# Pooled sums on VectorE alone, three products cut in two, and a new order of steps in a fused attention and two-mixer kernel

## The chip, the core and the metric

The kernel runs on one core of a Trainium2 chip. TensorE (PE), VectorE (DVE), ScalarE (ACT) and GpSimd (POOL) each work through a queue of their own in order; SyncE (SP) issues most DMA transfers, POOL the accumulating ones. Times are device microseconds of one execution; the kernel's time is the median of three.

## What is computed

Local and pooled attention on 4 batches of 8 heads, 576 positions and width 64, then a channel mix, then a gated layer with a convolution over three positions:

```python
q_d = q.reshape(B, H, Sd, factor, D).mean(axis=3)      # factor 4; k_d, v_d alike
out_d = sm_attn(q_d, k_d, v_d)
out_up = np.repeat(out_d, factor, axis=2)
mask = np.abs(pos[:, None] - pos[None, :]) < factor
scores = np.where(mask, scale * q @ k.T, -1e9)
x = out_up + softmax(scores) @ v

xk = mu_k * x + (1.0 - mu_k) * x_prev                  # xr alike, with mu_r
k = np.maximum(xk @ w_k, 0.0)
v = k * k @ w_v
x = sigmoid(xr @ w_r) * v

h = np.maximum(x @ w_in, 0.0)
conv_out = sum(conv_w[k] * hp[:, k:k + S, :] for k in range(3))
out = h * sigmoid(conv_out) @ w_out
```

The model is 512 wide and 1024 in the inner layer. All is float32.

## The kernel before

**Phase one.** Attention goes by groups of four heads (two groups a batch). A group of batch 0 is done in two halves (blocks 0 to 9 and 10 to 17), one of the later batches at once. Its steps are: load keys and queries (`kq`) and values (`vw`); sums of four neighbouring positions of keys and queries (`pooled_kq`, lines 501 to 525, tiles `kqd`); local scores (L549, L558) with maximum, exponential, sum and normalisation on DVE and ACT (L574 to L596); pooled scores (L623) with theirs (L640 to L667); transposes (L699, L750); outputs (L718, L769); and an addition of both on DVE (L784) that frees the PSUM bank of L769. PSUM for scores and outputs of attention is two tiles, `a20` and `a21`, used in turns.

The mix multiplies each chunk of positions by w_k and w_v. The first chunk (288 positions of batch 0) runs in plain f32 on weights as they arrive (L871 for w_k, L901 for w_v, on tiles `st_f`). For all later chunks each float32 operand is split into a rounded part and the rest, and a product is three matmuls (high by high, low by high, high by low): L935 with w_k, L985 with w_v. A weight tile is loaded in a transposed form of its bits: ACT cuts it (L398, L399), DVE puts it together (L380, L383), then its high part is written by ACT or DVE (L419 or L421, the function `high`) and its low part by DVE (L425). `mix_prep` makes the operand of a chunk (L832 on ACT, L840 on DVE, then the split at L849 and L854).

**Phase two** takes six chunks of 384 positions: gates with w_r (L1268), whose results are split into x1 (L1293 on ACT, L1295 on DVE), eight products with w_in (`hidden`, L1309; first result to ACT, L1337 to L1342), the convolution and its gate on DVE and ACT (L1354 to L1376), and the output with w_out (`outp`, L1389).

**What sets the order.** The program first records steps, each with an engine, what it reads and writes, and a function that issues its instructions. The list `ORDER` then gives the sequence in which all 1655 steps are issued, so it fixes each engine's queue and SP's and POOL's DMA queues too. `SECOND` names the steps that may run on two engines and take the second one: for the pooled sums of batches 1 to 3 `both = ("DVE", "POOL")`, for roundings and squares `("ACT", "DVE")`. Nine of the twelve pooled sums of batches 1 to 3 are in `SECOND`. On POOL such a sum is three additions:

```python
eng.tensor_tensor(out=o, in0=i[:, :, 0], in1=i[:, :, 1], op=ALU.add)
for j in range(2, FAC):
    eng.tensor_tensor(out=o, in0=o, in1=i[:, :, j], op=ALU.add)
```

Of the kernel before, what the change touches and what calls it, by code (L numbers as in the profile page):

```python
# [14 lines left out]
ALU = mybir.AluOpType  # L15
# [195 lines left out]
def pool(n):  # L211
    return 0.2 + 1.8e-3 * n
# [6 lines left out]
TAIL = 0.165  # L219
# [3 lines left out]
def tile_local_attention__then__channel_mix__then__conv_glu(  # L223
# [209 lines left out]
    def group(b, gp):  # L433
# [66 lines left out]
        def pooled_kq(i0, i1):  # L500
# [3 lines left out]
            for pr in range(2):  # L504
                t, k = g["kq"][0][:, pr], g["kq"][1]
                d, dk = g["kqd"][0][:, pr], g["kqd"][1]

                def f(eng, t=t, d=d):
                    o = d[:, a // FAC:e // FAC]
                    i = t[:, a:e].rearrange("p (s t) -> p s t", t=FAC)  # L510
                    if eng is nc.vector:
# [979 lines left out]
```

## Time and profile before

| | |
|---|---|
| median of 3 runs | 568.85 us (568.65 to 570.09) |
| the profiled execution | 568.25 us |
| its span in the trace | 566.5 us |
| PE busy | 547.7 us, 97% |
| DVE busy | 397.6 us, 70% |
| ACT busy | 307.2 us, 54% |
| POOL busy | 57.6 us, 10% |
| moved by DMA | 66.20 MB |

The span is the time from the first to the last instruction of one execution. The page of the profile also cuts the span into 40 slices of 14.16 us and gives for each the busy share of every engine and the granted clock of TensorE in tenths. A line of a timeline has the start, the time taken, the engine, the source line, the operation, the tiles written and read, the count, and in brackets the idle time ahead with what ended it. PE's waits give engine, line, what was waited for, the total, the times and the longest.

### The profile page before, as it was taken

What the parts mean: (1) busy time and instruction counts of PE and PEld (TensorE: products, weight loads), DVE (VectorE), ACT (ScalarE), POOL (GpSimd) and SP (SyncE); (2) the same over time, 40 slices, a digit from 0 to 9 for tenths busy, and PEclk for the clock granted to TensorE, in tenths of its full rate; (3) what the DMA queues carried; (4) which work ended last, traced back from release to release, by engine and by line L of the source; (5) the groups of instructions that cost most, each with busy time, mean ns of one, the idle gap of its engine ahead of it and who ended that gap; (6) DMA issues with size and microseconds to landing.
All of it is one profiled execution on the core that took longest, in us unless ns stands there. A gap on an engine that the chain in (4) does not pass through costs nothing.

```text
span 566.5 us, 13091 instructions
## 1 busy us (share of the span) xinstructions
PE 547.7 (97%) x5412; PEld 496.8 (88%) x5412; DVE 397.6 (70%) x758; ACT 307.2 (54%) x715; POOL 57.6 (10%) x159
## 2 busy tenths in 40 slices
PE   5898989999999999999999999999999999999996
PEld 3676768899988989999999998998998999999985
DVE  5989896774858575666456799677677777765770
ACT  4666866565644574663565764555445355453441
POOL 6023031511052100000000000000000000000000
PEclk9989997999999999999999999999999999999999
DMA  8545956383545373342205420303031200000011
GB/s 349 211 165 156 335 173 197 105 311 105 192 139 189 93 235 132 107 181 75 106 1 181 152 103 2 113 0 113 0 94 50 83 23 34 1 38 20 1 39 73
DMA packets 26396, 66.20 MB, mean 117 GB/s; under 512 B 2656, under 2 KB 12384, under 8 KB 25312
## 3 DMA queue, kind: packets, MB, share of 16 engines
q1 hardware_dynamic: 24608, 62.41, 31.5%
q0 software_dynamic: 1728, 2.95, 3.2%
q8 instruction: 42, 0.69, 0.5%
q14 instruction: 18, 0.15, 0.1%
HBM read 51.20 MB, written 14.16 MB: 115 GB/s over the span
## 4 chain that ended last, share of the span: by engine, by line
PE 78%; DVE 12%; DMA 3%; ACT 3%; issue 2%; POOL 1%; ACTq 0%; DVEq 0%; POOLq 0%; SPq 0%
PE a L1389 17%; PE mm L935 15%; PE mm L985 14%; PE mm L1309 8%; PE a L1309 8%; PE a L1268 5%; PE mm L1268 4%; DMA st_d<-in_moe_w_v 2%; PE a L769 2%; PE a L558 1%; PE a L750 1%; PE a L718 1%; PE a L699 1%; DVE st_f L380 1%; DVE st_f L383 1%
## 5 line engine op out<-in xcount | busy, mean ns | idle before, releaser
L1389 PE MATMUL a<-wk,wv 128*128 128x512 f32 x432 | 100.5, 390 | 0.0
L935 PE MATMUL mm<-xk,wk 128*128 128x432 f32 (+1 forms) x480 | 94.5, 353 | 0.7 <-ACT tmp L919 0.7
L1389 PEld LDWEIGHTS a<-wk,wv 128*128 128x128 f32 x432 | 81.0, 188 | 15.9
L985 PE MATMUL mm<-k,wv 128*128 128x432 f32 (+1 forms) x480 | 91.1, 347 | 0.0
L935 PEld LDWEIGHTS mm<-xk,wk 128*128 128x128 f32 x480 | 86.0, 193 | 4.5 <-ACT tmp L919 1.0
L985 PEld LDWEIGHTS mm<-k,wv 128*128 128x128 f32 x480 | 84.2, 188 | 3.6 <-issue 0.4
L1309 PE MATMUL mm<-k,wi 128*128 128x386 f32 x288 | 54.4, 340 | 0.7 <-ACT k L1293 0.7
L1309 PE MATMUL a<-k,wi 128*128 128x386 f32 x288 | 54.4, 340 | 0.0
L1309 PEld LDWEIGHTS mm<-k,wi 128*128 128x128 f32 x288 | 51.3, 189 | 1.9 <-ACT k L1293 1.0
L1309 PEld LDWEIGHTS a<-k,wi 128*128 128x128 f32 x288 | 51.4, 189 | 0.3
L1364 ACT ACTIVATE tmp<-tmp 128x384 f32<-128x384 f32 x48 | 24.8, 524 | 46.5 <-DVE tmp L1358 46.4
L954 ACT ACTIVATE tmp<-mm 128x432 f32<-128x432 f32 (+1 forms) x40 | 20.2, 508 | 25.4 <-PE mm L935 20.8
L380 DVE SCALAR_TENSOR_TENSOR st_f<-st_f,st_d 128x512 uint32<-128x512 uint32 x28 | 21.1, 752 | 18.2 <-ACT st_d L399 18.2
L1367 DVE SCALAR_TENSOR_TENSOR tmp<-tmp,h 128x384 f32<-128x384 f32 x48 | 26.3, 556 | 10.7 <-ACT tmp L1364 9.2
L1376 DVE TENSOR_TENSOR wv<-tmp,wv 128x384 fp32r<-128x384 f32 x48 | 25.9, 553 | 11.1 <-ACT wv L1374 11.0
L1374 ACT CAST wv<-tmp 128x384 fp32r<-128x384 f32 x48 | 24.0, 511 | 13.9 <-DVE tmp L1367 13.6
L1358 DVE SCALAR_TENSOR_TENSOR tmp<-h,cw_sb,tmp 128x384 f32<-128x384 f32 x48 | 29.7, 619 | 2.5
L974 DVE TENSOR_TENSOR k<-tmp,k 128x432 fp32r<-128x432 f32 (+1 forms) x40 | 22.8, 579 | 12.3 <-ACT k L966 11.6
L1355 DVE SCALAR_TENSOR_TENSOR tmp<-h,cw_sb,tmp 128x384 f32<-128x384 f32 x48 | 29.7, 619 | 2.5
L1268 PE MATMUL mm<-xk,wr 128*128 128x386 f32 x144 | 27.0, 340 | 0.3 <-ACT h L1337 0.3
L1268 PE MATMUL a<-xk,wr 128*128 128x386 f32 x144 | 26.7, 339 | 0.0
L1354 DVE TENSOR_SCALAR tmp<-h,cw_sb 128x384 f32<-128x384 f32 x48 | 20.0, 416 | 9.3 <-ACT h L1339 5.8
(165 smaller groups left out, 853.8 us busy)
## 6 DMA issues: line engine op xcount, KB each, us to landing
vw<-in_vw SPq DMA_DIRECT2D x7, 1152.0 KB, 9.0
kq<-in_kq SPq DMA_DIRECT2D x6, 1152.0 KB, 7.1
x_d<-xT SPq DMA_DIRECT2D x16, 288.0 KB, 5.6
out_dram<-xT SPq DMA_DIRECT2D x18, 256.0 KB, 2.0
st_d<-in_moe_w_k SPq DMA_DIRECT2D x8, 512.0 KB, 4.5
st_d<-in_moe_w_v SPq DMA_DIRECT2D x8, 512.0 KB, 5.4
st_d<-in_moe_w_in SPq DMA_DIRECT2D x8, 512.0 KB, 5.4
st_d<-in_moe_w_out SPq DMA_DIRECT2D x8, 512.0 KB, 3.9
```

Source lines behind the costliest of these rows:

```text
L380: nc.vector.scalar_tensor_tensor(out=f, in0=f, scalar=3, in1=low, op0=ALU.logical_shift_left, op1=ALU.bitwise_or)
L935: nc.tensor.matmul(pst[:, 0:n], lhsT=wk_t[wt][:, kt, mt * P:(mt + 1) * P], rhs=late["xk"][:, xs, kt, 0:n], start=(kt == 0 and g == 0), sto ...
L985: nc.tensor.matmul(pst[:, 0:n], lhsT=wv_t[wt][:, kt, mt * P:(mt + 1) * P], rhs=late["k2"][xs][:, at[kt], 0:n], start=(kt == 0 and g == 0), ...
L1268: nc.tensor.matmul(pst[:, 0:CW], lhsT=late["wr"][wt][:, kt, mt * P:(mt + 1) * P], rhs=r_t(xs)[:, kt, :], start=(kt == 0 and g == 0), stop= ...
L1309: nc.tensor.matmul(pst[:, 0:CW], lhsT=late["wi"][wt][:, kt, mt * P:(mt + 1) * P], rhs=x1s(xs)[:, kt, :], start=(kt == 0 and g == 0), stop= ...
L1355: nc.vector.scalar_tensor_tensor(out=cv, in0=tap(0), scalar=cw[:, 0, mt:mt + 1], in1=cv, op0=ALU.mult, op1=ALU.add)
L1358: nc.vector.scalar_tensor_tensor(out=cv, in0=tap(2), scalar=cw[:, 2, mt:mt + 1], in1=cv, op0=ALU.mult, op1=ALU.add)
L1364: step("ACT", act(CH), lambda: nc.scalar.activation(cv, cv, AF.Tanh, scale=0.5), (), [cvk])
L1367: lambda: nc.vector.scalar_tensor_tensor(out=gt, in0=cv, scalar=1.0, in1=tap(1), op0=ALU.add, op1=ALU.mult),
L1374: step("ACT", act(CH), lambda: nc.scalar.copy(gh, gf), ["wv_old", gk], [("gh", j)])
L1376: ("DVE",), (0.56,), lambda e: e.tensor_sub(gl, gf, gh.bitcast(F32)),
L1389: nc.tensor.matmul(pst, lhsT=xs[:, tt * P:(tt + 1) * P], rhs=wo[wt][:, kt, :], start=(kt == 0 and g == 0), stop=(kt == KF - 1 and g == 2),)
```

## The change

`pooled_kq` loses its form for POOL: all sums of four are one `reduce_sum` on DVE. In `hidden`, the products of chunk 0 with the first three blocks of w_in become two steps of six matmuls each (two rows of x1 each) in place of one of twelve. `ORDER` and `SECOND` are new; there are 1658 steps. Through `SECOND` other steps change their engine: up to the last operand of the first split product, the two copies of pooled v in batch 0, one square and seven roundings of weights go from DVE to ACT, and one rounding and one normalisation (L667) from ACT to DVE. The cost that the planner is told of one ACT step of the mix changes, its instruction doesn't.

```diff
 ORDER = [
-    88, 0, 78, 4, 1, 96, 5, 79, 65, 89, 80, 64, 66, 68, 69, 62, 90, 61, 67, 92, 8, 11, 12, 201, 13, 202, 10, 14,
...
+    0, 4, 80, 1, 88, 5, 96, 8, 64, 78, 11, 12, 10, 13, 62, 14, 66, 18, 79, 15, 69, 19, 25, 16, 20, 63, 24, 67,
...
 SECOND = {
-    3, 7, 22, 87, 100, 116, 124, 132, 140, 148, 168, 176, 190, 196, 226, 261, 266, 278, 279, 290, 314, 325, 365,
...
+    22, 92, 132, 168, 190, 256, 261, 290, 360, 365, 366, 375, 380, 385, 442, 451, 457, 461, 462, 467, 582, 587,
...
-                def f(eng, t=t, d=d):
-                    o = d[:, a // FAC:e // FAC]
-                    i = t[:, a:e].rearrange("p (s t) -> p s t", t=FAC)
-                    if eng is nc.vector:
-                        eng.reduce_sum(o, i, axis=AX.X)
-                    else:
-                        eng.tensor_tensor(out=o, in0=i[:, :, 0], in1=i[:, :, 1], op=ALU.add)
-                        for j in range(2, FAC):
-                            eng.tensor_tensor(out=o, in0=o, in1=i[:, :, j], op=ALU.add)
+                def f(t=t, d=d):
+                    nc.vector.reduce_sum(
+                        d[:, a // FAC:e // FAC], t[:, a:e].rearrange("p (s t) -> p s t", t=FAC), axis=AX.X
+                    )
...
-                if b:
-                    step(
-                        both, (0.15 + 1.05e-3 * (e - a), 3 * pool((e - a) // FAC)), f, [(k, i0)], ws,
-                        slack=SL[i0 > 0],
-                    )
-                else:
-                    step("DVE", 0.15 + 1.05e-3 * (e - a), lambda f=f: f(nc.vector), [(k, i0)], ws, slack=SL[i0 > 0])
+                step("DVE", 0.15 + 1.05e-3 * (e - a), f, [(k, i0)], ws, slack=SL[i0 > 0])
...
-            step("ACT", act(n) - 0.02 + 0.2 * (len(parts) - 1), scaled, xs + ["mus"], [tk])
+            step("ACT", act(n) + 0.1 + 0.3 * (len(parts) - 1), scaled, xs + ["mus"], [tk])
...
+        cut = KM // 2 if c == 0 and mt < 3 else KM
+        for k0 in range(0, KM, cut):
+            def f(k0=k0):
+                for kt in range(k0, k0 + cut):
...
+            us = 3 * cut * pe(CW) + TAIL
+            step(
+                "PE", us, f,
+                old + ["late", "mid"] + [(x, kt) for x in ("x1h", "x1l") for kt in range(k0, k0 + cut)]
+                + [("wi", x, 0, mt) for x in "hl"],
+                [pk], due=due(us),
+            )
```

In the changed program the source lines have numbers that are 3 to 11 lower (L512 is L509, L558 is L547, L901 is L890, L935 is L924, L1309 is L1301).

The beginning of DVE's queue. `st_f` and `st_d` are a weight tile, `kqd` the pooled sums, `kq` the first group, `kq_f` the second. Before:

```order
L380 SCALAR_TENSOR_TENSOR st_f1_114<-st_f1_114,st_d1_111 128x512
L383 SCALAR_TENSOR_TENSOR st_f1_114<-st_d1_111,st_f1_114 128x512
L512 TENSOR_REDUCE kqd0_127<-kq0_125 128x224
L512 TENSOR_REDUCE kqd0_127<-kq0_125 128x64 x2
L512 TENSOR_REDUCE kqd0_127<-kq0_125 128x224
L574 TENSOR_REDUCE sums0_141<-a20_177 128x2x5
L575 TENSOR_TENSOR probs0_133<-a20_177,sums0_141 128x2x5x38
L640 TENSOR_REDUCE sums1_142<-a21_178 128x2
```

Now:

```order
L509 TENSOR_REDUCE kqd0_127<-kq0_125 128x224 x2
L563 TENSOR_REDUCE sums0_141<-a20_177 128x2x5
L564 TENSOR_TENSOR probs0_133<-a20_177,sums0_141 128x2x5x38
L629 TENSOR_REDUCE sums1_142<-a21_178 128x2
L629 TENSOR_REDUCE sums1_142<-a21_178 128x1
L630 TENSOR_SCALAR sums1_142<-sums1_142 128x3
L579 TENSOR_REDUCE sums0_141<-probs0_133 128x10
L580 RECIPROCAL sums0_141<-sums0_141 128x10
L509 TENSOR_REDUCE kqd_f0_128<-kq_f0_126 128x224
```

The decoding of a weight tile that stood first has gone behind the first scores, and the two short sums (128x64) of the second half have gone with it.

POOL's queue behind its set-up: pooled sums (`kqd`) and the accumulating loads of pooled values (`vd`). Before:

```order
L514 TENSOR_TENSOR kqd0_127<-kq0_125 128x288
L516 TENSOR_TENSOR kqd0_127<-kqd0_127,kq0_125 128x288 x2
L375 DMA vd0_131<-in_vp 80x512
L514 TENSOR_TENSOR kqd0_127<-kq0_125 128x288
L516 TENSOR_TENSOR kqd0_127<-kqd0_127,kq0_125 128x288 x2
L375 DMA vd0_131<-in_vp 80x512 x3
L514 TENSOR_TENSOR kqd0_127<-kq0_125 128x288
L516 TENSOR_TENSOR kqd0_127<-kqd0_127,kq0_125 128x288 x2
```

Now, in DVE's queue, where both sums of batch 1's first group stand (`kqd0` from `kq0`, 128x288), from the one to just past the other:

```order
L509 TENSOR_REDUCE kqd0_127<-kq0_125 128x288
L656 TENSOR_TENSOR pd_f0_137<-pd_f0_137,sums3_144 128x288
L773 TENSOR_TENSOR xT0_119<-a20_177,od0_139 128x4x32 x2
L425 TENSOR_TENSOR wk1_116<-st_f0_113,wk0_115 128x4x128
```
```order
L380 SCALAR_TENSOR_TENSOR st_f0_113<-st_f0_113,st_d2_112 128x512
L383 SCALAR_TENSOR_TENSOR st_f0_113<-st_d2_112,st_f0_113 128x512
L425 TENSOR_TENSOR wk1_116<-st_ff0_145,wk0_115 128x4x128
L425 TENSOR_TENSOR wk1_116<-st_f1_114,wk0_115 128x4x128
L509 TENSOR_REDUCE kqd0_127<-kq0_125 128x288
L773 TENSOR_TENSOR xT0_119<-a21_178,od1_140 128x4x32 x2
```

The additions on POOL are gone and its loads follow one another; each sum is one reduce between the parts of batch 0's attention and the decoding of weights.

PE's queue ahead of the first split product (L935, now L924). `xT1` by `st_f` are the f32 products with w_v, `pt0` by `vw0` the outputs of batch 1's first group, `kqd0` the pooled scores of its second group. Before:

```order
L901 MATMUL mm1_174<-xT1_120,st_ff0_145 128x288 x4
L750 MATMUL a10_175<-ident_105,probs0_133 128x128 x4
L750 MATMUL a11_176<-ident_105,probs0_133 128x128 x4
L750 MATMUL a10_175<-ident_105,probs0_133 128x128
L901 MATMUL mm1_174<-xT1_120,st_ff1_146 128x288 x4
L769 MATMUL a20_177<-pt0_135,vw0_129 64x32 x36
L769 MATMUL a21_178<-pt0_135,vw0_129 64x32 x36
L623 MATMUL a20_177<-kqd0_127 32x144 x20
```

Now:

```order
L890 MATMUL mm0_173<-xT1_120,st_f0_113 128x288 x4
L707 MATMUL a11_176<-pdt0_138,vd0_131 64x160 x8
L739 MATMUL a10_175<-ident_105,probs0_133 128x128 x4
L739 MATMUL a11_176<-ident_105,probs0_133 128x128 x4
L739 MATMUL a10_175<-ident_105,probs0_133 128x128
L890 MATMUL mm1_174<-xT1_120,st_ff0_145 128x288 x4
L758 MATMUL a21_178<-pt0_135,vw0_129 64x32 x36
L890 MATMUL mm1_174<-xT1_120,st_ff1_146 128x288 x4
L890 MATMUL mm0_173<-xT1_120,st_f1_114 128x288 x4
L758 MATMUL a20_177<-pt0_135,vw0_129 64x32 x36
```

Both outputs stood next to each other, straight ahead of the pooled scores; now two f32 products stand between them, and the local scores of the second group (rows that follow) come ahead of its pooled scores.

## Rows read from the trace of the kernel before

**Rows 1.** The page, busy time by engine, and TensorE's granted clock by slice.

```profile
PE 547.7 (97%) x5412; PEld 496.8 (88%) x5412; DVE 397.6 (70%) x758; ACT 307.2 (54%) x715; POOL 57.6 (10%) x159
...
PEclk9989997999999999999999999999999999999999
```

**Rows 2.** Busy time by stretch: length, PE, PEld, DVE, ACT, POOL, clock, DMA share, GB/s.

```profile
10.00:90.00 80.00, 71.66 (x1384) 55.29 (x1375) 72.18 (x155) 55.72 (x147) 15.53 (x22) 0.93 0.64 210
100.00:200.00 100.00, 99.19 (x1684) 91.29 (x1683) 69.14 (x129) 55.35 (x149) 26.13 (x30) 1.00 0.53 163
24.00:26.00 2.00, 1.04 (x18) 0.82 (x17) 2.00 (x7) 1.50 (x5) 0.00 (x0) 1.00 0.72 213
82.00:84.00 2.00, 0.47 (x32) 0.47 (x34) 2.00 (x6) 1.87 (x5) 0.08 (x1) 1.00 0.52 81
88.00:90.00 2.00, 2.00 (x34) 1.72 (x40) 0.54 (x2) 1.96 (x11) 0.00 (x0) 0.50 0.03 10
```

**Rows 3.** PE's waits: two of them, in phase two.

```profile
PE mm L1309 <- ACT k L1293: 0.7, 1, 0.7
...
PE mm L1268 <- ACT h L1337: 0.3, 1, 0.3
```

**Rows 4.** DVE's timeline: steps that come to DVE or leave it.

```profile
17.45 0.74 DVE L496 COPY vd<-mm 80x256 f32<-80x256 f32 x2
...
39.39 0.45 DVE L892 TENSOR_TENSOR xT<-tmp 128x288 f32<-128x288 f32 x1
...
51.45 0.41 DVE L421 CAST wk<-st_ff 128x512 fp32r<-128x512 f32 x1
...
77.39 1.35 DVE L512 TENSOR_REDUCE kqd<-kq 128x288 f32<-128x1152 f32 x1
```

**Rows 5.** POOL's timeline, 30 to 40 us: two of a pooled sum's three additions.

```profile
35.84 2.67 POOL L516 TENSOR_TENSOR kqd<-kqd,kq 128x288 f32<-128x288 f32 x2
```

**Rows 6.** DVE's timeline, 34 to 48 and 78 to 82 us: instructions beside POOL's additions.

```profile
35.24 1.09 DVE L380 SCALAR_TENSOR_TENSOR st_f<-st_f,st_d 128x512 uint32<-128x512 uint32 x1 [0.66 <-ACT st_d L399]
36.37 1.34 DVE L383 SCALAR_TENSOR_TENSOR st_f<-st_d,st_f 128x512 uint32<-128x512 uint32 x1
...
44.28 0.77 DVE L596 TENSOR_TENSOR probs_f<-probs_f,sums 128x304 f32<-128x304 f32 x1
44.97 1.43 DVE L425 TENSOR_TENSOR wk<-st_ff,wk 128x512 fp32r<-128x512 f32 x1
46.32 1.16 DVE L421 CAST wk<-st_f 128x512 fp32r<-128x512 f32 x1
...
78.98 1.43 DVE L425 TENSOR_TENSOR wv<-st_f,wv 128x512 fp32r<-128x512 f32 x1
80.34 1.20 DVE L840 SCALAR_TENSOR_TENSOR tmp<-xT,mus,tmp 128x288 f32<-128x288 f32 x1
```

**Rows 7.** DVE's timeline: like instructions without POOL's additions.

```profile
38.37 0.48 DVE L596 TENSOR_TENSOR probs<-probs,sums 128x304 f32<-128x304 f32 x1
...
41.61 0.68 DVE L425 TENSOR_TENSOR wk<-st_ff,wk 128x512 fp32r<-128x512 f32 x1
42.21 0.68 DVE L380 SCALAR_TENSOR_TENSOR st_f<-st_f,st_d 128x512 uint32<-128x512 uint32 x1
42.93 0.69 DVE L383 SCALAR_TENSOR_TENSOR st_f<-st_d,st_f 128x512 uint32<-128x512 uint32 x1
...
76.96 0.51 DVE L840 SCALAR_TENSOR_TENSOR tmp<-xT,mus,tmp 128x288 f32<-128x288 f32 x1
```

**Rows 8.** The chain that ended last: start, time, twelve matmuls of L935 each.

```profile
86.61 3.25 PE mm L935 x12
...
90.72 2.28 PE mm L935 x12
...
101.88 1.60 PE mm L935 x12
```

**Rows 9.** ACT's timeline, 20 to 30 us: a rounding of a weight tile.

```profile
26.40 0.62 ACT L419 CAST wk<-st_f 128x512 fp32r<-128x512 f32 x1
```

More of the change, by code (lines that the diff above doesn't have):

```diff
@@ L1304, in hidden @@
         pst, pk = ring("mm2", mm2)
-        def f():
-            for kt in range(KM):
-                for g, (wt, xs) in enumerate(((0, 0), (1, 0), (0, 1))):
-                    nc.tensor.matmul(
-                        pst[:, 0:CW], lhsT=late["wi"][wt][:, kt, mt * P:(mt + 1) * P], rhs=x1s(xs)[:, kt, :],
-                        start=(kt == 0 and g == 0), stop=(kt == KM - 1 and g == 2),
-                    )
-        us = 12 * pe(CW) + TAIL
-        old = [("mm", pk[1]) if pk[1] < 2 else "a1_old"]
-        step(
-            "PE", us, f,
-            old + ["late", "mid"] + [(x, kt) for x in ("x1h", "x1l") for kt in range(KM)]
-            + [("wi", x, 0, mt) for x in "hl"],
-            [pk], due=due(us),
-        )
+        old = [("mm", pk[1]) if pk[1] < 2 else "a1_old"]
+        cut = KM // 2 if c == 0 and mt < 3 else KM
+        for k0 in range(0, KM, cut):
+            def f(k0=k0):
+                for kt in range(k0, k0 + cut):
+                    for g, (wt, xs) in enumerate(((0, 0), (1, 0), (0, 1))):
+                        nc.tensor.matmul(
+                            pst[:, 0:CW], lhsT=late["wi"][wt][:, kt, mt * P:(mt + 1) * P],
+                            rhs=x1s(xs)[:, kt, :],
+                            start=(kt == 0 and g == 0), stop=(kt == KM - 1 and g == 2),
+                        )
[5 more added lines that the diff above has]
+                [pk], due=due(us),
+            )
         i = count["h"] = count.get("h", -1) + 1
```

170 rows, old and new, of tables (ORDER, SECOND) are left out of this document.

## The prediction

> **What bounds the kernel now.** I read the page first. TensorE (PE) is busy for 547.7 of 566.5 us [rows 1], so all that any edit can win is in the 18.8 us where PE stands, and in stretches where its clock is low: the clock line reads 8 tenths in the slice from 28 to 42 us and 7 in that from 85 to 99 us. Next the table by stretches [rows 2]. From 100 to 200 us PE is busy for 99.19 of 100 us. From 10 to 90 us it is busy for 71.66 of 80, so 8.34 us are idle, and there VectorE (DVE) has only 80 - 72.18 = 7.82 us free, ScalarE (ACT) 80 - 55.72 = 24.28 us. The bound of that first stage (attention of batch 0, the first mix, the cutting of w_k and w_v) is therefore DVE's queue, with PE close behind it. Behind 90 us the kernel runs at PE's pace.
>
> The table's short rows show one thing more. From 24 to 26 us PE is busy for 1.04 of 2 us and from 82 to 84 us for 0.47, and soon after the second, from 88 to 90 us, the granted clock is 0.50, that is 1.2 GHz, the lower level [rows 2]. So an idle piece costs more than its own length.
>
> Of PE's waits I use two later ones [rows 3]: where phase two begins, 0.7 us for the split of x1 (L1293) and 0.3 us for L1337.
>
> **DVE's first stage, edit by edit.** Up to the last operand of the first split product (L935), the order gives DVE this:
>
> - Three pooled sums that GpSimd (POOL) did: both of batch 1's first group, and one of its second. One reduce over 1152 columns takes 1.35 us [rows 4], so +4.05 us.
> - Off DVE, to ACT: two copies of pooled v (0.74 us a pair), one square (0.45) and seven roundings of weights (L421, 0.41 each) [rows 4]: -(1.48 + 0.45 + 2.87) = -4.80 us. Back from ACT: one rounding (0.41) and one normalisation, about as long as the square (0.45): +0.86.
> - With POOL's adds gone, DVE's own instructions keep their normal length. While POOL adds (one pair of adds took 2.67 us [rows 5]), seven DVE instructions were stretched [rows 6] against like ones outside [rows 4, 7]: 1.09 - 0.68, 1.34 - 0.69, 0.77 - 0.48, 1.43 - 0.68, 1.16 - 0.41, 1.43 - 0.68, 1.20 - 0.51, together 0.41 + 0.65 + 0.29 + 0.75 + 0.75 + 0.75 + 0.69 = 4.29 us. -4.29.
>
> The sum is +4.05 - 4.80 + 0.86 - 4.29 = -4.18 us on the queue that bounds the stage.
>
> The seven rows show DVE late by 0.29 to 0.75 us each. The Trainium skill (SBUF — State Buffer, Who interferes with whom) says that the two engines share ports, that a DVE instruction with two inputs in SBUF contends with a GpSimd one that reads it, that the loser blocks for the whole instruction, and that a reduce never contends on this chip. By it each of the seven could have lost up to a whole add, and the gain would be larger; the measured excess decides here, and no run yet shows the reduce beside POOL's work.
>
> What can eat the 4.18 us: the end of DVE's queue is what PE waits for before L935, and PE has 8.34 idle us ahead of it [rows 2], so PE can move up by as much. Bounds: 0, if PE's own f32 products are what sets the pace; and 4.18 plus all the 7.82 us of DVE's idle time, if the new order also closes its gaps. I take 4.2: it is the nearest to rows, and I see no reason in the order for the gaps to grow.
>
> **The start.** The keys and queries are now loaded ahead of the first tile of w_k, and DVE no longer begins with decoding one (L380 and L383, 0.68 + 0.69 us [rows 7]). The scores can start earlier by 0 (if the load lands no earlier) to 1.4 us. The decode comes later in the same queue, so the queue's sum is unchanged; I take 0 and keep 1.4 for the low end.
>
> **The entry of the first split product.** Before, PE ran the outputs L769 of both pairs and then waited for DVE's adds to free a bank. Now two f32 products with w_v stand between these steps. They are work that PE has anyway, so the sum of PE's work is unchanged and the idle piece of 82 to 84 us, 2 - 0.47 = 1.53 us, is filled; this is part of the 8.34 us and not counted again. The slow stretch behind it is what matters: two sets of twelve products took 3.25 and 2.28 us, and at full clock 1.60 each [rows 8], so 2.3 us hang on it. I put that into a rival, as I can't say from the order alone that no other idle piece comes in its place.
>
> **Six more pooled sums** fall between 90 and 185 us: +8.1 us for DVE there. From 100 to 200 us DVE has 30.86 us free while PE is full [rows 2], so I cost them at 0. If the cover goes, a sum ahead of a score product costs up to its 1.35 us each, 8.1 in all. The DVE items that change sides with ACT behind 90 us have the same cover. Sums, maps of roundings and squares are in a fixed order on each queue, so what stands behind a late one waits too: the attention of batch 2 is earlier in PE's queue now, and its PE steps would stand first.
>
> **Phase two.** Three products with w_in are cut in two; the first halves need only the first two rows of x1, and all three stand in front of the second halves. Half a product is about 1.1 us of PE's work, so some 3.2 us lie under the split of the last x1, whose wait was 0.7; the other wait of 0.3 lies in the row of products that is now dealt anew [rows 3]. The cut adds no instruction. Term: -1.0; bounds 0 and -1.0, as the waits can't become less than nothing. The last three output tiles end as before. The changed cost of a step in the mix is a number for the planner and no instruction.
>
> **The sum.** The profiled execution took 568.25 us (span 566.5). 568.25 - 4.2 - 1.0 = 563.05. The median of the runs shown, 568.85, is 0.6 above that execution, so 563.65; I say 563.7.
>
> **The rivals.**
>
> *The slow clock goes too.* If no idle piece of PE like that from 82 to 84 us is left, the products behind it run at 2.4 GHz: another 2.3 us, and up to 1.4 from the start: 563.7 - 2.3 = 561.4, with both 560.0. For it: the two f32 products that now stand in the gap. Against: DVE still ends that stage, so PE's idle time, some 4 us of it, has to lie somewhere. The Trainium skill (TensorE: Matmul & The Clock Gate, HAM oscillation) says that gaps drop the clock again and that keeping PE supplied avoids it; by this trace the two idle pieces [rows 2] agree. Chance 0.22.
>
> *Nothing is returned.* The three sums are real work on DVE, 4.05 us. If the stretched instructions were slow for another reason (the DMAs that land at that time, say), the 4.29 us stay and DVE's queue is 4.05 - 4.80 + 0.86 = 0.1 longer. Then only phase two's 1.0 is left: 568.85 - 1.0 + 0.1 = 567.9, within the noise. Against: the seven lie where POOL adds, and like instructions on either side do not. The Trainium skill (VectorE: DVE Perf Modes, Rules for kernel authors) calls this reduce the slowest operation of the engine and advises against it on a hot path; by it this rival is the likelier, and the 1.35 us [rows 4] shows no fast form either. Chance 0.14.
>
> *ScalarE takes DVE's place: slower.* Place: 10 to 90 us. ACT gets seven roundings at 0.62 us [rows 9], a square like DVE's at 0.45 and copies like DVE's for 1.48, and gives back 0.62 + 0.45: 4.34 + 0.45 + 1.48 - 1.07 = 5.2 us more. ACT's queue is in order, and each cut of a weight tile (L398, L399) waits in it behind copies that wait for PE; if a cut comes later than DVE reaches its decode, DVE's 4.2 us are spent waiting, and ACT's 5.2 are added: 568.85 + 5.2 - 1.0 = 573.1. It decides from the point at which ACT's 24.28 free us [rows 2] are used up by such waits, about four fifths of them, as 5.2 are work. For it: the roundings are put right behind decodes. Against: so much free time. Chance 0.14.
>
> **How the numbers follow.** Forecast 0.50 (561.5 to 566.5), the slow clock 0.22, nothing returned 0.14, ScalarE 0.14. A measurement of this kernel tells 0.3% from no change, that is 1.7 us: below 567.1 is faster, above 570.6 slower. Faster gets the first two and a hundredth of the third's low side, 0.73; same 0.13; slower 0.14. The range reaches from 559.0 (both gains of the first rival and 1 us of DVE's gaps) to 569.5 (all of nothing returned, and the beginning of the slower case); outside lie most of ScalarE's case and the far end of a closed queue, together some 0.2.
>
> **What would show it.** Right: no POOL adds; L425, L380 and L421 at their short lengths everywhere; the first L935 at about 82.5 us where it stood at 86.61 [rows 8]; no wait for L1293; DVE still with free time from 100 to 200 us and PE still at 99. Wrong: DVE instructions of 1.1 us and more without POOL; or DVE's free time up in 10 to 90 us by as much as its work shrank, with waits for ACT's cuts ahead of it; or PE idle behind 90 us in front of the scores or transposes of batch 2. The split products starting as late as before would refute the main term whatever the end time is.

## The result, and the profile after

The changed kernel takes **563.86 us** (median of 6 runs, 562.78 to 565.08) where the kernel before takes 569.10 us (6 runs); the ratio is 0.9912, 95% interval 0.9887 to 0.9936. Run a second time, beside the experiments, it gave 0.9924 (0.9898 to 0.9950). The forecast of 563.7 us is met. Its main step is not met: the gain did not arrive where the text put it, and it exists only where edits that I costed apart from each other come together.

The profiled execution took 565.01 us (span 563.1), 3.2 us less than that of before; it is the second longest of its six. Two lines of the page:

```profile
PE 546.0 (97%) x5412; PEld 495.0 (88%) x5412; DVE 393.9 (70%) x757; ACT 307.1 (55%) x716; POOL 29.5 (5%) x132
...
PEclk9989998999999999999999999999999999999999
```

The table by stretches, the same five stretches as [rows 2] (columns as there):

```profile
10.00:90.00 80.00, 72.32 (x1363) 54.97 (x1362) 70.74 (x151) 60.26 (x158) 5.75 (x10) 0.96 0.68 228
100.00:200.00 100.00, 100.00 (x1765) 92.78 (x1764) 67.70 (x126) 56.51 (x148) 9.00 (x12) 1.00 0.55 169
24.00:26.00 2.00, 1.49 (x41) 1.19 (x43) 2.00 (x7) 1.08 (x6) 0.00 (x0) 1.00 0.49 150
82.00:84.00 2.00, 1.26 (x94) 1.15 (x80) 2.00 (x6) 1.36 (x3) 0.83 (x1) 1.00 0.35 88
88.00:90.00 2.00, 2.00 (x10) 2.00 (x10) 1.59 (x3) 1.08 (x2) 0.00 (x0) 0.50 0.99 396
```

From 10 to 90 us PE is idle for 7.68 us, against 8.34 before. I had forecast some 4 us less. Where the 3.4 us of span went shows when the first 400 us are cut in three (behind them PE is idle for as long as before); first before, then after:

```profile
0.00:30.00 30.00, 22.59 (x568) 15.93 (x569) 22.36 (x54) 17.79 (x46) 8.72 (x41) 0.95 0.69 265
30.00:100.00 70.00, 64.91 (x1028) 52.63 (x1028) 61.05 (x119) 48.34 (x124) 16.82 (x18) 0.92 0.67 212
100.00:400.00 300.00, 298.22 (x3000) 279.40 (x2999) 206.88 (x382) 166.99 (x381) 29.05 (x63) 1.00 0.38 123
```

```profile
0.00:30.00 30.00, 22.00 (x569) 14.95 (x570) 21.88 (x54) 18.27 (x49) 8.18 (x41) 0.98 0.70 266
30.00:100.00 70.00, 65.90 (x1104) 52.53 (x1103) 60.81 (x120) 52.10 (x134) 6.07 (x8) 0.96 0.69 231
100.00:400.00 300.00, 299.52 (x2943) 282.44 (x2942) 204.87 (x384) 165.87 (x378) 12.16 (x48) 1.00 0.37 119
```

PE's idle time changes by +0.59, -0.99 and -1.30 us, together -1.7. The other 1.7 us are PE's busy time (547.7 to 546.0): the same 5412 products, with less of them at 1.2 GHz. In this pair the clock stood at 0.50 for 13.65 us before and 6.82 us after:

```profile
26.89:33.72 6.83, 6.83 (x136) 5.42 (x129) 5.61 (x17) 3.06 (x9) 0.00 (x0) 0.50 0.45 147
84.92:91.74 6.82, 6.17 (x160) 5.65 (x161) 4.72 (x13) 4.89 (x19) 0.77 (x1) 0.50 0.23 52
```

```profile
28.86:32.27 3.41, 3.41 (x43) 2.46 (x21) 3.31 (x11) 2.54 (x8) 0.00 (x0) 0.50 0.51 151
86.88:90.29 3.41, 3.41 (x17) 3.41 (x16) 2.93 (x6) 1.08 (x2) 0.00 (x0) 0.50 0.97 318
```

That half is not steady. The six executions have mean granted clocks from 0.989 to 0.997; the three at 0.996 and 0.997 have spans of 560.9 to 561.2 us, the other three 562.5 to 563.2. When the changed kernel was run again, its median clock was 0.992, below the 0.994 of the kernel before beside it, and the ratio was 0.9924 all the same. So the clock moves single executions by about 2 us, and is not what the change brings: among all executions on record with a mean granted clock of 0.992 to 0.994, the median is 567.64 us before (31 executions) and 564.51 us after (7).

**VectorE's queue shrank by what the sum said.** Before, the last cut of xk, on which the first split product rests, ends at 85.86 + 0.89 = 86.75 us; after, at 82.95 + 0.45 = 83.40. VectorE's busy time up to there falls by 74.79 - 70.55 = 4.24 us (forecast: 4.18; how far that is luck is said below). The operand itself comes only 3.35 us earlier: VectorE's time without work up to there went from 11.96 to 12.85 us.

```profile
0.00:86.75 86.75, 74.25 (x1446) 56.07 (x1446) 74.79 (x158) 57.88 (x144) 23.40 (x57) 0.95 0.67 227
```

```profile
0.00:83.40 83.40, 73.56 (x1498) 54.25 (x1499) 70.55 (x151) 60.42 (x152) 13.44 (x48) 0.98 0.70 243
```

**PE did not take it.** Its waits, which answer to [rows 3], and its timeline at the place where the first split product (now L924) was to begin at 82.5 us:

```profile
PE a L547 <- issue: 2.4, 1, 2.4
...
PE a L707 <- ACT pdt L694: 1.5, 2, 1.3
...
PE mm L1301 <- ACT k L1282: 0.4, 1, 0.4
```

```profile
82.80 0.46 PE L547 MATMUL a<-kq 64*32 64x38 f32 x24
85.61 0.29 PE L547 MATMUL a<-kq 64*32 64x38 f32 x11 [2.35 <-issue]
85.83 0.41 PE L924 MATMUL mm<-xk,wk 128*128 128x288 f32 x1
```

The first split product begins at 85.83 us, 0.8 us earlier than before [rows 8], though its operands were there at 83.40. In its way stands the second half of the scores of batch 1's second group (L547), which the new order puts ahead of it, and inside that a stop of 2.35 us for which the profile names no other engine ("issue"). I had not seen that coming.

### The profile page after: what moved, and what is told of

It is laid out like the page before. It is cut to its first block, busy times and chain, and to the rows that moved or that the text cites. A ratio compares the mean times of both kernels' runs of the same rounds, so it can differ in the third digit from the quotient of the medians.

```text
span 563.1 us, 13038 instructions
## 1 busy us (share of the span) xinstructions
PE 546.0 (97%) x5412; PEld 495.0 (88%) x5412; DVE 393.9 (70%) x757; ACT 307.1 (55%) x716; POOL 29.5 (5%) x132
## 4 chain that ended last, share of the span: by engine, by line
PE 90%; DMA 3%; DVE 2%; ACT 2%; issue 1%; SPq 0%; ACTq 0%; DVEq 0%
PE a L1381 18%; PE mm L924 16%; PE mm L974 16%; PE a L1301 9%; PE mm L1301 9%; PE a L1257 5%; PE mm L1257 5%; PE a L758 3%; PE mm L860 2%; DMA vw<-in_vw 2%; PE a L707 2%; PE a L547 1%; PE a L739 1%; PE a L688 1%; DMA st_d<-in_moe_w_v 1%; PE mm L890 1%
## 5 line engine op out<-in xcount | busy, mean ns | idle before, releaser
L924 PE MATMUL mm<-xk,wk 128*128 128x432 f32 (+1 forms) x480 | 93.9, 353 | 0.0
L924 PEld LDWEIGHTS mm<-xk,wk 128*128 128x128 f32 x480 | 85.7, 192 | 3.7 <-issue 0.5
L1301 PE MATMUL mm<-k,wi 128*128 128x386 f32 x288 | 54.3, 340 | 0.5 <-ACT k L1282 0.4
L1301 PE MATMUL a<-k,wi 128*128 128x386 f32 x288 | 54.4, 340 | 0.0
L1301 PEld LDWEIGHTS mm<-k,wi 128*128 128x128 f32 x288 | 51.3, 189 | 1.5 <-ACT k L1282 0.8
L1301 PEld LDWEIGHTS a<-k,wi 128*128 128x128 f32 x288 | 51.5, 189 | 0.5
L380 DVE SCALAR_TENSOR_TENSOR st_f<-st_f,st_d 128x512 uint32<-128x512 uint32 x28 | 19.2, 684 | 12.4 <-ACT st_d L399 12.3
L908 ACT COPY tmp<-mm 128x432 f32<-128x432 f32 (+1 forms) x24 | 11.5, 480 | 28.4 <-PE mm L974 16.4
```

Source lines behind the costliest of these rows:

```text
L924: nc.tensor.matmul(pst[:, 0:n], lhsT=wk_t[wt][:, kt, mt * P:(mt + 1) * P], rhs=late["xk"][:, xs, kt, 0:n], start=(kt == 0 and g == 0), sto ...
L1301: nc.tensor.matmul(pst[:, 0:CW], lhsT=late["wi"][wt][:, kt, mt * P:(mt + 1) * P], rhs=x1s(xs)[:, kt, :], start=(kt == 0 and g == 0), stop= ...
```

## The experiments

Ratios are to the kernel before, run beside each. "Busy" is VectorE's busy time up to the end of the last cut of xk that the first split product needs, "operand" the time of that end, "product" the start of the first split product, all from the one profiled execution. (The first products of a set need only the first rows of xk, so "product" can lie a little ahead of "operand".)

| kernel | median us | ratio (95%) | busy | operand | product |
|---|---|---|---|---|---|
| before | 568.19 to 569.10 | 1 | 74.79 | 86.75 | 86.61 |
| changed | 563.86 | 0.9912 (0.9887 to 0.9936) | 70.55 | 83.40 | 85.83 |
| changed, again | 564.57 | 0.9924 (0.9898 to 0.9950) | 70.56 | 84.28 | 86.24 |
| engines alone | 569.13 | 1.0024 (1.0003 to 1.0044) | 71.14 | 86.39 | 86.25 |
| order alone | 571.56 | 1.0053 (1.0032 to 1.0074) | 76.46 | 87.79 | 89.59 |
| nine sums back on POOL | 567.75 | 0.9987 (0.9973 to 1.0002) | 72.74 | 88.39 | 90.19 |
| three sums back on POOL | 568.57 | 1.0011 (0.9985 to 1.0037) | 72.59 | 87.00 | 88.75 |
| other moves undone | 567.44 | 0.9973 (0.9957 to 0.9990) | 73.45 | 85.00 | 87.07 |
| scores apart | 565.11 | 0.9953 (0.9926 to 0.9979) | 70.65 | 83.00 | 82.33 |
| scores apart, 403 | 564.53 | 0.9913 (0.9887 to 0.9940) | 70.45 | 83.20 | 82.52 |

### Engines alone, order alone

The kernel before with the changed kernel's choice of engines, all pooled sums on VectorE among it, in its own order:

```diff
 SECOND = {
-    3, 7, 22, 87, 100, 116, 124, 132, 140, 148, 168, 176, 190, 196, 226, 261, 266, 278, 279, 290, 314, 325, 365,
+    22, 92, 132, 168, 190, 256, 261, 290, 360, 365, 366, 375, 380, 385, 442, 451, 457, 461, 462, 467, 582, 587,
...
```

> The kernel before in its own order and with uncut products; only the choice of engines is the changed kernel's: nine pooled sums on VectorE, and the copies, squares and roundings that change sides. Theory A (VectorE's queue of the first stage shrinks by about 4 us because POOL's adds no longer stretch its instructions): VectorE's busy time up to the last operand of the first split product falls from 76.1 us to about 72, that operand comes about 3 us before 86.7 us, and the time falls by 2 to 4 us, to 565 to 567. Theory B (the new order makes the gain, the choice of engines none): 568 to 570, the first split product at about 86.6 us as before.

Measured: ratio 1.0024, the time of theory B. Theory A's work is there (busy 74.79 to 71.14, -3.65 us; up to that operand the trace has 74.79 where the expectation says 76.1) and its gain is not: the operand comes 0.36 us earlier. VectorE waits instead. Its waits up to there, before and then here (line numbers are one less):

```profile
DVE st_f L380 <- ACT st_d L399: 5.4, 2, 4.7
DVE st_ff L380 <- ACT st_d L399: 1.9, 3, 1.3
...
DVE xT L784 <- PE a L769: 0.2, 1, 0.2
```

```profile
DVE st_f L379 <- ACT st_d L398: 5.0, 2, 4.8
DVE st_ff L379 <- ACT st_d L398: 3.7, 4, 1.6
DVE xT L783 <- PE a L768: 1.4, 2, 1.0
```

VectorE waits 1.4 us more for ACT's cuts of the weights and 1.2 more for PE's outputs. The longest wait for a cut behind the first 30 us, 1.6 us where that tile cost no wait before, goes through ACT to the load of the tile. The cut of that tile, before and then here, and VectorE's decode of it here:

```profile
73.65 0.66 ACT L398 ACTIVATE st_ff<-st_d 128x512 f32<-128x512 f32 x1 [0.67 <-DMA st_d<-in_moe_w_v]
```

```profile
74.18 0.67 ACT L397 ACTIVATE st_ff<-st_d 128x512 f32<-128x512 f32 x1 [2.30 <-DMA st_d<-in_moe_w_v]
75.45 0.69 DVE L379 SCALAR_TENSOR_TENSOR st_ff<-st_ff,st_d 128x512 uint32<-128x512 uint32 x1 [1.62 <-ACT st_d L398]
```

ACT itself stands for 2.30 us until the tile has landed, 0.5 us later than before. In the old order VectorE reaches this decode sooner, and the weights don't come sooner. VectorE waits for cuts, as the rival said that put ScalarE in VectorE's place, but here it is the load that is late and not ACT's own work. Behind 100 us, PE then waits 1.7 us for ACT's pooled probabilities and 2.2 us in phase two, where the products are uncut.

The reverse, the changed order and cut with the engines of before:

```diff
 SECOND = {
-    22, 92, 132, 168, 190, 256, 261, 290, 360, 365, 366, 375, 380, 385, 442, 451, 457, 461, 462, 467, 582, 587,
+    3, 7, 22, 87, 100, 116, 124, 132, 140, 148, 168, 176, 190, 196, 226, 261, 266, 278, 279, 290, 314, 325, 365,
...
```

> The changed order and the cut products, with the engines of the kernel before (nine pooled sums on POOL, all choices as before). Theory A: instructions of VectorE beside POOL's adds are stretched again by 0.3 to 0.75 us each, the last operand of the first split product comes 2 to 4 us later than the changed kernel's 83.4 us, and since 2.4 us of that lie under PE's stall in the scores, the time is 564 to 566.5. Theory B: the order alone gives the gain: 563 to 564.5, as the changed kernel.

Measured: ratio 1.0053, slower than before, which neither theory had. The direction is A's: the operand comes at 87.79 us. So each half alone loses, 0.2% and 0.5%, and the two together win 0.8 to 0.9%.

### Which choice of engines pays, in the new order

The pooled sums back on POOL: all nine, and then the three of the first stage alone (the adds that the change took out are put in again).

```diff
 SECOND = {
...
+    278, 279, 314, 496, 497, 532, 642, 643, 677,
...
```

> The changed kernel with the nine pooled sums back on POOL and nothing else undone. Theory A (POOL's adds stretch VectorE's instructions by as much as the sums cost on VectorE): VectorE's busy time in the first 83 us changes by less than 1 us, the last operand of the first split product comes within 1 us of 83.4, and the time is within 1 us of the changed kernel's, 563 to 565. Theory C (POOL's work is free for VectorE): VectorE gives up three sums, 4.05 us, the operand comes at about 80 us, and the time is 561 to 563, limited by PE's stall. Theory D (the stretching is worth much more than the sums): 566 and more.

```diff
 SECOND = {
...
+    278, 279, 314,
...
```

> The changed kernel with only the three pooled sums of the first stage (batch 1) back on POOL; the six later ones stay on VectorE. If the price of POOL's adds lies in the first stage, where VectorE bounds: the last operand of the first split product comes at 87 to 88.5 us instead of 83.4 to 84.3, as with all nine on POOL, and the ratio is that run's, 0.997 to 1.0. If it lies in the six later sums (POOL's queue, its loads of pooled v, contention behind 90 us): the ratio is the changed kernel's, 0.990 to 0.994.

Measured: 0.9987 and 1.0011. The time with nine, 567.75 us, is that of theory D; the operand comes at 88.39 us with nine and at 87.00 with three. With three the gain is gone as with nine, so the six later sums cost and give nothing that can be measured, and the three of the first stage are worth the distance from 0.9924 to 1.0011, nearly 5 us (the two intervals do not meet). Theory A of the run with nine expected VectorE's busy time unchanged. With three sums taken off it, which fill 3 x 1.26 = 3.78 us of it, it is 2.04 us longer (72.59 against 70.55). POOL's adds thus stretch VectorE's instructions by 5.8 us, in this order more than the 4.29 that I had counted in the old one. Seven instructions have nearly all of it. Four of them, from the run with three sums; POOL first, then VectorE:

```profile
51.47 0.98 POOL L514 TENSOR_TENSOR kqd<-kq 128x288 f32<-128x288 f32 x1
52.52 2.62 POOL L516 TENSOR_TENSOR kqd<-kqd,kq 128x288 f32<-128x288 f32 x2
...
77.77 0.99 POOL L514 TENSOR_TENSOR kqd<-kq 128x288 f32<-128x288 f32 x1
78.84 2.63 POOL L516 TENSOR_TENSOR kqd<-kqd,kq 128x288 f32<-128x288 f32 x2
```

```profile
51.07 1.94 DVE L425 TENSOR_TENSOR wk<-st_ff,wk 128x512 fp32r<-128x512 f32 x1
52.93 1.43 DVE L425 TENSOR_TENSOR wk<-st_f,wk 128x512 fp32r<-128x512 f32 x1
...
77.48 1.83 DVE L380 SCALAR_TENSOR_TENSOR st_f<-st_f,st_d 128x512 uint32<-128x512 uint32 x1
79.35 1.31 DVE L383 SCALAR_TENSOR_TENSOR st_f<-st_d,st_f 128x512 uint32<-128x512 uint32 x1
```

In the changed kernel the same L425 pair takes 0.69 and 0.68 us:

```profile
49.82 0.69 DVE L425 TENSOR_TENSOR wk<-st_ff,wk 128x512 fp32r<-128x512 f32 x1
50.42 0.68 DVE L425 TENSOR_TENSOR wk<-st_f,wk 128x512 fp32r<-128x512 f32 x1
```

Against these, and against the usual 0.69 us of L380 and L383 [rows 7], the excesses are 1.25, 0.75, 1.14 and 0.62 us, beside adds of about 1.0 and 1.3 us. The loads and the order are the same in both kernels, so it is the adds that do it.

The other half of the choice, all sums on VectorE and the rest as before:

```diff
 SECOND = {
-    22, 92, 132, 168, 190, 256, 261, 290, 360, 365, 366, 375, 380, 385, 442, 451, 457, 461, 462, 467, 582, 587,
+    3, 7, 22, 87, 100, 116, 124, 132, 140, 148, 168, 176, 190, 196, 226, 261, 266, 290, 325, 365, 366, 370, 375,
...
```

> The changed kernel with all pooled sums on VectorE, but every copy, square and rounding on the engine that it had before; in the first stage VectorE gets back 4.80 us and gives 0.86 us. Prediction's term: VectorE's busy time up to the last operand of the first split product rises from 73.0 to about 76.9 us, the operand comes at 86 to 88 us, and since PE's stall of about 2 us in the scores then lies beside it or behind it, the ratio is 0.995 to 1.000. Rival (ACT was in VectorE's way in the first stage, so that giving it less work pays): the operand stays at 83.4 to 84.3 us and the ratio at 0.990 to 0.994.

Measured: 0.9973, about 2.8 us slower than the changed kernel (0.9924; again the intervals do not meet). VectorE's busy time rises by 2.90 us where the term said 3.94; the operand comes 0.7 to 1.6 us later, less than said, as VectorE's own waits shrink. The moves to ACT pay, in this order.

### The stop in the scores

The changed kernel unaltered, beside the others:

> The changed kernel unaltered, as the measure for the experiments of the same chip. All theories: the ratio of its first runs again, 0.989 to 0.994; the 2.35 us in which PE stands in the middle of the scores of batch 1's second group are there again at 83 us, within 0.7 us, if they come from the number of small instructions ahead of them, and are gone or elsewhere if they were an accident of that execution.

Measured: 0.9924. The stop is there again, 1.9 us, and a new wait besides:

```profile
PE a L707 <- DMA vd<-in_vp: 2.2, 1, 2.2
PE a L547 <- issue: 1.9, 1, 1.9
PE a L707 <- ACT pdt L694: 1.7, 2, 1.5
```

Now the scores' second half (316) behind the first split product (363):

```diff
 ORDER = [
...
-    312, 177, 352, 316, 182, 353, 322, 363, 323,
+    312, 177, 352, 182, 353, 322, 363, 316, 323,
...
```

> The changed kernel with one step moved on PE: the second half of the scores of batch 1's second group stands behind the first split product instead of ahead of it. Theory F (the 2.35 us in which PE stands in the middle of those scores, with nothing that the profile names, come from 500 small instructions in 4 us, more than PE's instructions are brought in): the stall goes or falls below 0.5 us, the first split product starts at about 83.5 us instead of 85.8, the slow stretch from 86.9 to 90.3 us goes or not, and the time is 2 to 4 us under the changed kernel's, 560 to 562. Theory G (these scores wait for an operand or a bank that the profile leaves out): they wait as long in their new place, and the time stays at 563 to 564.5.

Measured: the stop is gone, and the product begins at 82.33 us, about the 82.5 that the prediction gave. In the changed kernel PE issues 251 products and 250 weight loads in the 4 us ahead of the stop, here 200 and 198 ahead of the product:

```profile
79.20:83.20 4.00, 4.00 (x251) 3.43 (x250) 3.78 (x10) 2.63 (x7) 0.94 (x2) 1.00 0.49 109
```

```profile
78.30:82.30 4.00, 4.00 (x200) 3.13 (x198) 3.81 (x11) 2.63 (x7) 0.91 (x2) 1.00 0.57 160
```

All eight profiles in which those scores directly follow the others have the stop (1.7 to 2.4 us); the four with a product between have 0.3 us or none. So the run of small products causes it. Theory G's late operand is excluded: here these scores end at 85.0 us, before the 85.6 at which they go on in the changed kernel.

The traces also show what PE waits for. The profile lists DMA packets of instructions, and on queue q8 each kernel has 42 of them for its 10824 products and weight loads, one for some 258. One is under way when the stop of the changed kernel begins (from 82.3 to 84.1 us, 5.7% of 16 engines' time, that is 1.65 us):

```profile
q8 instruction: 1, 0.02, 5.7%
```

It lands at 84.01 us, and PE goes on at 85.61. In all eight profiles such a packet is under way when the stop begins, and PE goes on 1.3 to 1.6 us after it has landed. The five other stops of PE over 0.2 us that the profile calls "issue" behind 30 us, each 0.3 to 0.4 us long, end 1.2 to 1.5 us behind such a packet. So theory F's cause holds: the small products are used up faster than the next instructions come in.

The other half of theory F failed: 565.11 us, ratio 0.9953, no better than the changed kernel. What came in place of the stop:

```profile
PE a L705 <- DMA vd<-in_vp: 4.4, 1, 4.4
PE a L686 <- DVE pd L654: 1.5, 1, 1.5
PE a L705 <- ACT pdt L692: 1.0, 1, 1.0
```

PE comes 1.5 us too early for VectorE's normalisation of the pooled scores, and at 113 us it comes before batch 2's pooled values are loaded. The twelve executions reach from 562.91 to 569.83 us (the profiled one is the longest), as if that load came in time in some and not in others. Next a product with w_v (403) was moved ahead of those outputs as well:

```diff
 ORDER = [
...
-    502, 512, 399, 510, 425,
+    502, 512, 399, 403, 510, 425,
...
-    431, 520, 403, 518, 528,
+    431, 520, 518, 528,
...
```

> The changed kernel with the second half of those scores behind the first split product, as in the run before, and one product with w_v of batch 1 moved ahead of the pooled outputs of batch 2, which waited 4.4 us there for their values in the profiled execution of that run. Theory F with the late load as its price: all executions lie at 560.5 to 563, without the group of executions at 567 to 570, and the ratio is 0.987 to 0.991, below the changed kernel's. Rival: the load is late by more than one product (1.9 us): a second group of executions stays, and the ratio is 0.991 to 0.996.

Measured: 0.9913, between the two theories; six executions from 563.50 to 565.52 us, none over 567. The wait for the load is 0.8 us, that for VectorE still 1.5. Then a product with w_k (373) for that one:

```diff
 ORDER = [
...
-    325, 319, 326, 359, 328, 365, 373, 329,
+    325, 319, 373, 326, 359, 328, 365, 329,
...
```

> The kernel with the scores' second half behind the first split product and one product with w_v ahead of the pooled outputs, and one product with w_k more moved: it stands ahead of the transposes of batch 1's second pooled group, which waited 1.5 us there for VectorE's normalisation once the stall was gone. If that wait took the stall's place and nothing else does: PE's idle time up to 100 us falls from 11.5 to about 10 us, and the ratio to 0.987 to 0.991. If another wait comes (the pooled values, a bank), the ratio stays at 0.991 to 0.993.

Measured: 0.9941 (0.9917 to 0.9964), 564.51 us. The 1.5 us are gone, and PE waits 3.5 us for ACT's transposed pooled probabilities (two waits, the longest 2.1). Then that wait by itself, in the changed kernel: ACT's cut of a weight tile (187), which waits for its load, behind the two copies (292, 294) that PE needs:

```diff
 ORDER = [
...
-    283, 187, 284, 192, 175, 271, 292, 269, 168, 169, 294, 170,
+    283, 284, 192, 175, 271, 292, 269, 168, 169, 294, 187, 170,
...
```

> The changed kernel with one step moved on ACT: the cut of a tile of w_v (0.69 + 0.56 us, and 1.6 us of waiting for its load ahead of it) stands behind the two copies of the transposed pooled probabilities instead of ahead of them. Theory H (ACT's queue holds PE there): PE's wait of 1.3 us at 68 us goes, and the time falls by 0 to 1.3 us, as PE's stall in the scores at 83 us may take it up. Rival I (VectorE needs that cut): VectorE's decode of the same tile comes 1.4 us later, the last operand of the first split product too, and the time rises by 0 to 1.4 us.

Measured: PE's wait of 1.3 us is gone, as theory H has it, and the operand is no later (83.16 us); the ratio is 0.9898 with an interval from 0.9863 to 0.9934, which tells nothing apart. Last, all these moves together, and batch 2's pooled outputs later:

```diff
 ORDER = [
...
-    503, 513, 400, 401, 532, 515, 514, 527, 406, 516,
+    503, 400, 401, 532, 515, 406, 516, 513, 514, 527,
...
```

> All moves so far together (scores' second half, two products, ACT's cut behind the two copies), and the pooled outputs of batch 2 one product and one set of transposes later, so that the load of pooled values has some 4 us more. If the waits found (2.4, 1.5, 1.3 and up to 4.4 us) are the first stage's remaining ones: no wait of PE over 1 us between 30 and 200 us, and the ratio is 0.984 to 0.989. If VectorE's queue itself still sets the stage, PE's waits for VectorE take their place and the ratio is 0.989 to 0.993.

Measured: 0.9919 (0.9899 to 0.9940), 563.69 us, inside the rival's range. PE's idle time from 30 to 100 us is 2.83 us where the changed kernel has 4.10, but one wait over 1 us is left, again for ACT's pooled probabilities (1.4 us). None of these kernels is shown to beat the changed one.

### The cut products

The three products with w_in whole again:

```diff
-        cut = KM // 2 if c == 0 and mt < 3 else KM
-        for k0 in range(0, KM, cut):
-            def f(k0=k0):
-                for kt in range(k0, k0 + cut):
+        def f():
+            for kt in range(KM):
...
```

> The changed kernel with the three products with w_in whole again, each where its second half stood. Prediction's term: the wait of 0.7 us for the split of x1 and 0.3 us behind it come back, so 0.7 to 1.0 us more than the changed kernel. Rival: the cut is worth nothing, because the wait was a matter of where phase one's end left VectorE: within 0.3 us of the changed kernel.

Measured: 0.9949 (0.9923 to 0.9974); its interval overlaps that of the changed kernel, so the time decides nothing. The wait does, with 1.2 us here against the 0.4 us above; the longer of the two, 0.8 us where phase two begins, is the one that the cut removes, and the other is in both kernels:

```profile
PE mm L1337 <- ACT k L1280: 1.2, 2, 0.8
```

## Why the prediction was right, and where it was not

**The total** is right: -5.2 us forecast, -5.2 us between the medians of six executions each. Beside the experiments the kernel before ran 87 times, with a median of 568.34 us; the changed kernel's 14 executions have 564.48. By these the change is worth 3.9 us.

**The main term, -4.18 us.** Its price for POOL's adds is right. In the old order with the new engines, six of the seven stretched instructions still stand on VectorE, and without the adds they take 3.53 us less, where the term has 3.54 for them. Two of them, which took 1.09 and 1.43 us [rows 6]:

```profile
34.97 0.69 DVE L379 SCALAR_TENSOR_TENSOR st_f<-st_f,st_d 128x512 uint32<-128x512 uint32 x1 [0.20 <-ACT st_d L398]
...
46.07 0.69 DVE L424 TENSOR_TENSOR wk<-st_ff,wk 128x512 fp32r<-128x512 f32 x1
```

That the sum meets the measured 4.24 us to 0.1 us is in part luck. It adds up whole rows, and rows that follow each other overlap by some 0.08 us, so that a pooled sum of 1.35 us fills 1.26 of VectorE's time (the changed kernel):

```profile
77.36 1.35 DVE L509 TENSOR_REDUCE kqd<-kq 128x288 f32<-128x1152 f32 x1
78.62 0.82 DVE L843 TENSOR_TENSOR xk<-tmp,xk 128x288 fp32r<-128x288 f32 x2
```

With the new engines in the old order busy time falls by 3.65 us, and only with the new order by 4.24. In the new order the parts differ from their costs: the three sums on VectorE are worth 2.04 us of its busy time where the term has 4.29 - 4.05 = 0.24, and the other moves 2.90 where it has 3.94.

Two things in the term were wrong. The sum was worked out from instructions, without the order. "I see no reason in the order for the gaps to grow": they grew by 0.9 us in the change, and with the same engines in the old order by 3.3 us (11.96 to 15.25), which ate nearly the whole term. And the text says that split products starting as late as before would refute the term whatever the end time is: they started 0.8 us earlier, not 4.1. As a time at PE the term is refuted at that place. The runs show how the 0.8 comes about: the new order alone puts the product 3.0 us later (86.61 to 89.59), and the new engines in that order 3.8 us earlier (85.83). Taking the scores apart brought the product to 82.33 us, but not the end of the kernel down.

**"PE can move up by as much"**, as it has 8.34 idle us ahead. A good part of these lies ahead of 30 us, where loads and first scores set the pace (7.41 us from 0 to 30 before, 8.00 after). From 30 to 100 us there were 5.09, and the change took 0.99 of them; the kernel with four moves, 2.26.

**The moves to ACT** were costed at what VectorE sheds. In the new order they are worth 2.8 us of time; in the old order, where they were run only together with the sums, nothing was won. Price and order could not be separated, and the new order is the part of which the prediction said least. It pays with these engines: with those of before it is 3.0 us slower than before.

**Six later sums at 0:** right within the noise. VectorE is free for 32.3 of the 100 us from 100 to 200 and PE is full; three or nine sums on POOL make no measurable difference. One of the later sums had held PE up on POOL, for 0.29 us at 170 us.

**Phase two, -1.0:** the two waits of 0.7 and 0.3 us [rows 3] are both gone; the 0.3 is gone with whole products too, so that part is the order's. A new one has come further on, so the balance is -0.6, and "no wait for L1293" (now L1282) did not hold:

```profile
357.53 1.79 PE L1301 MATMUL mm<-k,wi 128*128 128x386 f32 x7 [0.44 <-ACT k L1282]
```

Every profile with the new order has this wait, with cut or whole products, and neither of the two with the old order has it.

**The start, 0:** PE's idle time up to 30 us went from 7.41 to 8.00 us in the one profile of the changed kernel and to 7.04 in the other; no gain that stays.

**What made the total fit.** In the profiled pair the main term's missing time is filled by 1.7 us of clock and by 0.8 us of PE's waits from 100 to 200 us ([rows 2]: 0.81 us idle, none after), neither of them in the sum. The rival "the slow clock goes too" came half true in that pair and not at all in the second set of runs. "So an idle piece costs more than its own length" does not always hold: the stop in the scores is followed within 2 us by a granted clock of 0.50 in five of the eight profiles that have it, and in three, with stops of 1.7 to 1.9 us, it is not. The pair lies 3.2 us apart, the medians of six 5.2 and all executions 3.9; so most of the gap between pair and medians is spread between executions, and where the rest lies, in executions without a trace, stays open.

**The rivals.** "Nothing is returned" is excluded by the sums put back. "ScalarE takes DVE's place" did not come: ACT's busy time from 10 to 90 us rises by 4.5 us (5.2 forecast) and leaves it 19.7 us free. The Trainium skill (VectorE: DVE Perf Modes, Rules for kernel authors) calls the reduce the slowest operation of VectorE and advises to consider another form on a hot path; here the hot path was better off with 1.35 us of reduce than beside adds on POOL. The Trainium skill (SBUF — State Buffer, Who interferes with whom) calls the shared ports an exclusive lock, and says of VectorE's two-port modes that the one who comes second is blocked for the whole instruction. The excesses of 0.62 to 1.25 us fit, as none is longer than an add of 1.3 us, but they don't show who blocked whom.

## What to carry to other kernels

Work taken off the engine that bounds a stage shortens the stage only if the order lets the engines around it deliver sooner: price a new assignment of engines and a new order together, and test each alone before crediting either. Count what a neighbour on another engine costs by comparing like instructions with and without it; here three sums on POOL cost VectorE 5.8 us of stretching and saved it 3.8. And when a total comes out as forecast, look at the place that the forecast named before believing its steps.

## What was not expected

Some 500 small products and weight loads in 4 us end in a stop of PE of 1.7 to 2.4 us, while some 400 in 4 us do not. It appeared in all eight profiles with that run of steps, and went, or shrank to 0.3 us, when one set of large products (1.9 us) stood in its midst. Each stop ends 1.3 to 1.6 us after a packet of instructions has landed, so a long run of small products can be limited by how fast its instructions come in. And the load of pooled values, for which PE waits nowhere in the profile before, held it up for 0, 0.8, 2.2 or 4.4 us, from 113 to 115 us on, in profiles with a quicker first stage.
